# A linear-attention block and a dropless mixture of experts on one core: expert capacity goes from 512 slots each to 896 slots for a pair

## The chip, the cores and the metric

The kernel runs on one core of one Trainium2 chip. The metric is the time of one execution on the device in microseconds, taken over several runs. TensorE (PE in the rows, PEld for its weight loads) does the matrix products, VectorE (DVE), ScalarE (ACT) and GpSimd (POOL) the elementwise work, and SyncE (SP) issues the plain DMAs. GpSimd issues the DMAs whose rows are picked by an index tile.

## The reference, cut to what matters

```python
# gated linear attention: B=4, H=8, S=768, D=48
for t in range(S):
    state = alpha[:, :, t, :, None] * state + k_t (outer) v_t
    y[:, :, t] = einsum('bhd,bhde->bhe', q[:, :, t], state)
x = y.transpose(0, 2, 1, 3).reshape(3072, 384)
# mixture of experts, top 1: E=8, F=1024
expert_idx = argmax(x @ w_gate, axis=1)
gate_w     = softmax(x @ w_gate)[expert_idx]
for e in range(8):                      # rows of expert e only
    h[rows_e]  = maximum(x[rows_e] @ w1[e], 0)    # 384 -> 1024
    y2[rows_e] = h[rows_e] @ w2[e]                # 1024 -> 384
out = gate_w[:, None] * y2
```

For the inputs that are drawn (a fixed seed), the reference gives the eight experts 420, 387, 356, 354, 404, 409, 352 and 390 tokens.

## The kernel before

The program has two stages. The first runs over 24 chunks of 128 tokens: it loads alpha, k, q and v, forms the attention rows as products on TensorE, writes them with their negated logits to a DRAM tensor (`x_rows`), and counts each token into a slot of its expert. Each chunk's steps are issued by hand in a software pipeline (`for s in range(-5, NT + 1)`). `choose` marks the expert of each token of a group of chunks (one to four chunks) in `oh`, `ohs` keeps the running sum over chunks, and `rank_products` and `slots_of` turn them into slot numbers. The slot numbers become one-hot matrices whose products (`tokens_of_slots`) give, for each slot, the number of its token; `indices` makes the index tile `g_idx` of them.

The second stage has the experts. Each has 4 blocks of 128 slots (`NJ = 4`, `CAP = 512`), filled or not; an unused slot points at a row of zeros. For each expert in turn TensorE does three things:

- `turn`: the gathered rows `xg` of a block (128 tokens x 384) are transposed in three 128x128 pieces into a PSUM tile `xtp` (two of them in turn), and VectorE copies it to `xgT`. This is done for the expert that comes next, between the two layers of the present one.
- `layer1`: 8 blocks of hidden units, each 3 products with 512 columns of `xgT` moving (`hp`), then a ReLU on VectorE or ScalarE in turn.
- `layer2`: for each of the 4 token blocks, 8 products in which `w2` moves with 384 columns and 128 columns of `h` are the stationary operand (`zp`); ScalarE scales by the gate, and GpSimd writes the rows out by index.

An f32 product shows as two MATMUL rows in the trace (192 products of layer 1 before: 366 rows with 512 columns and 36 with 256, some for each half of a product that is split in two). The order on each engine is the order of the code (`tc.manual_schedule`). In it `gates` (the gate weights of an expert: two operations on VectorE, an exponential on ScalarE, three more on VectorE) stands ahead of `turn`. For the first expert `begin` does two turns, the first half of three products, then two more turns. The weights come in tiles with three buffers, `w1` and `w2` of an expert 1.5 MB each; those of expert e+3 are requested once `layer2` of e is issued.

Tokens beyond the 512 slots of an expert go to overflow blocks, which a loop after the experts runs one by one (`extra_blocks` sets its count, which is zero when no expert has more than its capacity).

Of the kernel before, what the change touches and what calls it, by code (L numbers as in the profile page):

```python
# [18 lines left out]
def kernel(  # L19
# [22 lines left out]

    nc = tc.nc
    B, H, S, D = q.shape
    C = 128
# [13 lines left out]
    NJ = 4  # L59
    CAP = NJ * C  # L60
    NX = -(-(N - CAP) // C)
    NC = E * NT
    NXB = NT - NJ

# [37 lines left out]
    for name, shape, dt, pattern, base, mult in (  # L102

        ("first_w", [C, E], F32, [[-1, E]], E, 0),

        ("oh_base", [C, E], F16, [[NT, E]], 0, 0),
# [3 lines left out]
        ("thr", [C, NXB], F32, [[C, NXB]], CAP, 0),  # L110
        ("kx", [1, NX], F32, [[1, NX]], 0, 0),
        ("slot_e", [C, E], F32, [[NT * C, E]], 0, 0),
# [4 lines left out]
    first_w, oh_base, iota_h, tokv, thr, kx, slot_e = (iotas[n][1] for n in iotas)  # L117

    def late_consts(i):
# [10 lines left out]
        if i in (2, 3):  # L130
            for ti, tf, pattern, base, mult in list(iotas.values())[4 * (i - 2) : 4 * (i - 1)]:
                nc.gpsimd.iota(ti[:], pattern=pattern, base=base, channel_multiplier=mult)
                nc.gpsimd.tensor_copy(tf[:], ti[:])
            if i == 2:

                nc.sync.dma_start(x_d[N : N + 1, :], zero_w[:])
# [18 lines left out]
    def fetch(ex):  # L155
        w1 = wpool.tile([C, DB, F], F32, name="w1")
        w2 = wpool.tile([C, FB, Dm], F32, name="w2")
        nc.sync.dma_start(w1[:], moe_w1[bass.ds(ex, 1)].rearrange("e (a p) f -> p (e a) f", p=C))
        nc.sync.dma_start(w2[:], moe_w2[bass.ds(ex, 1)].rearrange("e (a p) d -> p (e a) d", p=C))
        return w1, w2  # L160


    with tc.tile_pool(name="ld", bufs=6) as ld, \
# [148 lines left out]
        def choose(g):  # L312
# [8 lines left out]
            nc.vector.tensor_tensor(oh[:, t, :], sc[:], top[:].unsqueeze(2).to_broadcast([C, n, E]), op=ALU.is_equal)  # L321
            for s in g:
                if s == 0:
                    nc.gpsimd.tensor_copy(ohs[:, 0, :], oh_base[:])
                nc.gpsimd.tensor_add(ohs[:, s + 1, :], ohs[:, s, :], oh[:, s, :])
# [8 lines left out]
        def slots_of(g, pos):  # L334
# [5 lines left out]
            with nc.allow_low_precision("a single number is not zero, and it is an integer"):  # L340
                nc.vector.reduce_sum(slot_i[:], own[:], axis=AX)
# [24 lines left out]
        def indices(blocks):  # L366

            n = len(blocks)
            tv = route[:, :NC].rearrange("p (e b) -> p e b", e=E)[:, :, blocks[0] : blocks[-1] + 1]
            gv = g_idx[:].rearrange("p (e b) -> p e b", e=E)[:, :, blocks[0] : blocks[-1] + 1]  # L370
            up = work.tile([C, E, n], F32, name=f"up{n}", bufs=1)
# [19 lines left out]
        for s in range(-5, NT + 1):  # L391
# [27 lines left out]
            if s == 15:  # L419
                w_t[0] = fetch(0)  # L420
# [7 lines left out]
        indices(range(NJ))  # L428
        indices(range(NJ, NT))
# [4 lines left out]
    xg_pool = ctx.enter_context(tc.tile_pool(name="moe_x", bufs=3))  # L434
# [3 lines left out]
    def extra_blocks():  # L438

        cnt = sm.tile([C, E], F32)  # L440
        nc.vector.tensor_tensor(cnt[:], tot[:], slot_e[:], op=ALU.subtract)
        og = sm.tile([C, E, NXB], F32)
        nc.vector.tensor_tensor(
            og[:], cnt[:].unsqueeze(2).to_broadcast([C, E, NXB]), thr[:, None, :].to_broadcast([C, E, NXB]), op=ALU.is_gt,
# [4 lines left out]
        nc.vector.tensor_tensor_scan(ove[:], ovt[:], zero_e[:], 0.0, op0=ALU.add, op1=ALU.add)  # L449
        ended = sm.tile([1, NX, E], F32)  # L450
        ove_b = ove[0:1, None, :].to_broadcast([1, NX, E])
        nc.vector.tensor_tensor(ended[:], ove_b, kx[0:1, :].unsqueeze(2).to_broadcast([1, NX, E]), op=ALU.is_le)
        xf = sm.tile([1, 2 * NX + 1], F32)
        nc.vector.reduce_sum(xf[:, :NX], ended[:], axis=AX)
        nc.vector.tensor_tensor(ended[:], ended[:], ove_b, op=ALU.mult)
        nc.vector.reduce_max(xf[:, NX : 2 * NX], ended[:], axis=AX)
        nc.vector.tensor_scalar_min(xf[:, :NX], xf[:, :NX], float(E - 1))
        nc.vector.tensor_tensor(xf[:, NX : 2 * NX], kx[0:1, :], xf[:, NX : 2 * NX], op=ALU.subtract)
        nc.vector.scalar_tensor_tensor(
            xf[:, NX : 2 * NX], in0=xf[:, :NX], scalar=float(NT), in1=xf[:, NX : 2 * NX], op0=ALU.mult, op1=ALU.add,  # L460
        )
        nc.vector.tensor_scalar(
            xf[:, NX : 2 * NX], xf[:, NX : 2 * NX], scalar1=float(NJ), scalar2=float(NC - 1), op0=ALU.add, op1=ALU.min,
        )
# [3 lines left out]
    def gather(g):  # L468
        g["xg"] = xg_pool.tile([C, NJ, W], F32, name="xg")
        for j in range(g["n"]):  # L470
            nc.gpsimd.indirect_dma_start(  # L471
                out=g["xg"][:, j, :], out_offset=None,
                in_=x_d[:, :], in_offset=bass.IndirectOffsetOnAxis(ap=g["gi"](j), axis=0),
            )

    def gates(g):

        n = g["n"]
        lg = g["xg"][:, :n, Dm:]
        low = wk.tile([C, NJ], F32, name="low")  # L480
        nc.vector.tensor_reduce(low[:, :n], lg, axis=AX, op=ALU.min)
        ex = wk.tile([C, NJ, E], F32, name="ex")
        nc.vector.tensor_tensor(ex[:, :n, :], low[:, :n].unsqueeze(2).to_broadcast([C, n, E]), lg, op=ALU.subtract)
        nc.scalar.activation(ex[:, :n, :], ex[:, :n, :], AF.Exp)
        g["gw"] = wk.tile([C, NJ], F32, name="gw", bufs=3)
        nc.vector.reduce_sum(g["gw"][:, :n], ex[:, :n, :], axis=AX)
        nc.vector.tensor_scalar_add(g["gw"][:, :n], g["gw"][:, :n], 1e-9)
        nc.vector.reciprocal(g["gw"][:, :n], g["gw"][:, :n])

    def turn(g, blocks=None):  # L490
        if blocks is None or blocks[0] == 0:
# [119 lines left out]
```

## Time and profile before

| what | value |
|---|---|
| time, median of 3 runs | 533.97 us (533.76 to 534.03) |
| the profiled execution, its own time | 535.65 us |
| span of that execution | 533.8 us |
| TensorE busy | 498.4 us, 93% of the span |
| weight loads on TensorE | 314.5 us, 59% |
| VectorE, ScalarE, GpSimd busy | 144.4, 107.3, 145.5 us |

The span is what the trace covers; the profiled execution's own time is 1.85 us longer, and 1.68 us above the median of the runs. The attention stage ends near 155 us in the span, the experts begin after a gap at about 166 us, and run to the end.

### The profile page before, as it was taken

To read this page: it belongs to the slowest core of one execution; us is meant where nothing else is said; L and a number is where in the kernel's file an instruction comes from. 1 tells how busy PE (TensorE), PEld (TensorE's weight loads), DVE (VectorE), ACT (ScalarE), POOL (GpSimd) and SP (SyncE) were. 2 spreads that over 40 slices of the span, in tenths; PEclk is the share of its full clock that TensorE was granted. 3 is DMA by queue.
4 is the path that set the end of the run, shared out by engine and by line. 5 is a ranking of instruction groups with operands and counts; after the bars stand their busy time and mean duration, and the time that the engine had idled before them with its cause. 6 is when DMAs were issued, how large, how long until landed. Compare 5 with 4: busy or idle time off the path is not lost.

```text
span 533.8 us, 7442 instructions
## 1 busy us (share of the span) xinstructions
PE 498.4 (93%) x2893; PEld 314.5 (59%) x2893; DVE 144.4 (27%) x399; ACT 107.3 (20%) x217; POOL 145.5 (27%) x229
## 2 busy tenths in 40 slices
PE   4999999999985999999999999999999999999992
PEld 1888888888873645445545544544654554454451
DVE  2435666756782130113012012012001101201100
ACT  3544545444210001010010110101010010011110
POOL 4567454565426201401310130130130010020011
PEclk9999999999995999999999999999999999999997
DMA  8999998889914230503323053050232000000000
GB/s 170 201 186 217 199 217 181 169 262 300 346 47 121 75 114 35 193 9 129 108 100 125 35 178 119 29 190 17 121 136 69 16 29 3 2 33 8 1 29 17
DMA packets 127726, 60.58 MB, mean 113 GB/s; under 512 B 110624, under 2 KB 121951, under 8 KB 127690
## 3 DMA queue, kind: packets, MB, share of 16 engines
q1 hardware_dynamic: 114818, 48.87, 34.0%
q0 software_dynamic: 4096, 11.15, 6.2%
q10 hardware_dynamic: 8776, 0.08, 0.9%
q8 instruction: 24, 0.39, 0.3%
q14 instruction: 12, 0.10, 0.0%
HBM read 50.51 MB, written 11.14 MB: 115 GB/s over the span
## 4 chain that ended last, share of the span: by engine, by line
issue 57%; PE 26%; POOL 10%; DVE 2%; DMA 2%; SPq 1%; ACT 0%; POOLq 0%; ACTq 0%
POOL out_dram L536 6%; PE sA L241 4%; PE y L267 4%; POOL xg L471 4%; PE xr L300 4%; PE tp L228 4%; PE y L261 4%; PE cum L197 3%; PE kvp L278 2%; SPq L181 1%; PE hp L512 1%; DMA a_sb<-in_alpha_dram 1%; DMA xg<-x_rows,g_idx 1%; DMA Eb<-decay_rows 0%; DVE yT L282 0%
## 5 line engine op out<-in xcount | busy, mean ns | idle before, releaser
L512 PE MATMUL hp<-xgT,w 128*128 128x512 f32 (+1 forms) x402 | 169.4, 582 | 1.4 <-DVE xgT L497 1.4
L530 PE MATMUL zp<-w,h_sb 128*128 128x384 f32 x512 | 166.4, 486 | 0.0
L530 PEld LDWEIGHTS zp<-w,h_sb 128*128 128x128 f32 x512 | 96.7, 190 | 66.2 <-issue 0.5
L512 PEld LDWEIGHTS hp<-xgT,w 128*128 128x128 f32 x402 | 78.3, 195 | 89.4 <-issue 83.7
L536 POOL DMA_INDIRECT out_dram<-zo,g_idx x32 | 31.8, 995 | 291.1 <-ACT zo L535 264.8
L506 DVE TENSOR_SCALAR h_sb<-hp 128x512 f32<-128x512 f32 x32 | 22.1, 692 | 261.5 <-PE hp L512 261.5
L535 ACT ACTIVATE zo<-zp,gw 128x384 f32<-128x384 f32 x32 | 18.6, 581 | 166.2 <-PE zp L530 161.6
L508 ACT ACTIVATE h_sb<-hp 128x512 f32<-128x512 f32 x32 | 19.1, 597 | 160.3 <-PE hp L512 160.3
L471 POOL DMA_INDIRECT xg<-x_rows,g_idx x32 | 30.9, 967 | 11.9 <-issue 9.4
L197 PE MATMUL cum<-ln,cmask 128*128 128x384 f32 x48 | 24.1, 586 | 7.9 <-ACT ln L186 4.4
L241 PE MATMUL sB<-qT,kT 48*128 48x128 f32 x192 | 27.7, 285 | 0.0
L241 PE MATMUL sA<-qT,kT 48*128 48x128 f32 x192 | 27.7, 285 | 0.0
L496 PE MATMUL xtp<-ident,xg 128*128 128x128 f32 x96 | 15.4, 291 | 13.1 <-DVE xgT L497 8.6
L228 PEld LDWEIGHTS tp<-ident,kqb 128*128 128x128 f32 x192 | 23.0, 144 | 7.8 <-issue 4.8
L248 POOL TENSOR_SCALAR_AFFINE_SELECT dB<-dB 128x512 f32<-128x512 f32 x24 | 15.3, 638 | 39.9 <-ACT dB L247 26.4
L267 PE MATMUL y<-dB,vb 128*64 128x128 f32 x192 | 26.1, 279 | 0.0
L267 PE MATMUL y<-dA,vb 128*64 128x128 f32 x192 | 26.1, 279 | 0.0
L220 POOL TENSOR_TENSOR kqb<-k_sb,icp 128x384 f32<-128x384 f32 x24 | 24.1, 1002 | 7.4 <-ACT icp L200 7.3
L228 PE MATMUL tp<-ident,kqb 128*128 128x128 f32 x192 | 25.9, 280 | 0.1
L300 PE MATMUL xr<-back,yT 128*128 128x104 f32 x192 | 25.1, 274 | 0.6 <-DVE yT L282 0.4
L241 PEld LDWEIGHTS sA<-qT,kT 48*128 48x128 f32 x192 | 23.1, 187 | 2.5 <-issue 0.3
L221 POOL TENSOR_TENSOR kqb<-q_sb,cp 128x384 f32<-128x384 f32 x24 | 24.0, 1001 | 0.0
(106 smaller groups left out, 414.3 us busy)
## 6 DMA issues: line engine op xcount, KB each, us to landing
w<-in_moe_w_dram SPq DMA_DIRECT2D x16, 1536.0 KB, 7.1
x_rows<-xs SPq DMA_DIRECT2D x24, 196.0 KB, 2.8
a_sb<-in_alpha_dram SPq DMA_DIRECT2D x24, 192.0 KB, 4.0
k_sb<-in_k_dram SPq DMA_DIRECT2D x24, 192.0 KB, 3.8
q_sb<-in_q_dram SPq DMA_DIRECT2D x24, 192.0 KB, 3.8
vb<-in_v_dram SPq DMA_DIRECT2D x24, 192.0 KB, 4.0
Eb<-decay_rows ACTq DMA_DIRECT2D x40, 0.8 KB, 3.1
xg<-x_rows,g_idx POOLq DMA_INDIRECT x32, 3.7
```

Source lines behind the costliest of these rows:

```text
L197: nc.tensor.matmul(cum[:], lhsT=cmask[:], rhs=d["ln"][:], start=True, stop=True)
L220: nc.gpsimd.tensor_tensor(kq[:, 0, :, :D], d["k"][:], heads(d["icp"]), op=ALU.mult)
L221: nc.gpsimd.tensor_tensor(kq[:, 1, :, :D], d["q"][:], heads(d["cp"]), op=ALU.mult)
L228: nc.tensor.transpose(tp[:, p, :], pair(kqb[s % 4][:, i], p), ident[:])
L241: nc.tensor.matmul(t[:, p, :], lhsT=d["kT"][r : r + D, p, :], rhs=d["qT"][r : r + D, p, :], start=True, stop=True,)
L267: nc.tensor.matmul(y[r : r + DP, p, :], lhsT=d["v"][:, 2 * p + i, :], rhs=d["d" + "AB"[i]][:, p, :], start=(c == 0 and p == 0), stop=True, ...
L300: nc.tensor.matmul(xr[:, p, :], lhsT=d["yT"][:, p, :], rhs=back[:, p, :], start=True, stop=True)
L471: nc.gpsimd.indirect_dma_start(out=g["xg"][:, j, :], out_offset=None, in_=x_d[:, :], in_offset=bass.IndirectOffsetOnAxis(ap=g["gi"](j), ax ...
L506: nc.vector.tensor_relu(g["h"][:, f, :cols], hp[:, :cols])
L512: nc.tensor.matmul(hp[:, c0:c1], lhsT=g["w"][0][:, a, f * C : (f + 1) * C], rhs=g["xT"][:, a, c0:c1], start=(a == 0), stop=(a == DB - 1), ...
L530: nc.tensor.matmul(zp[:], lhsT=g["h"][:, f, j * C : (j + 1) * C], rhs=g["w"][1][:, f, :], start=(f == 0), stop=(f == FB - 1),)
L536: ins = nc.gpsimd.indirect_dma_start(out=out[:, :], out_offset=bass.IndirectOffsetOnAxis(ap=g["gi"](j), axis=0), in_=zo[:], in_offset=None ...
```

## The change

Experts are taken in pairs. A pair has 7 blocks of 128 slots (`NJ = 7`); each expert of it has 448 slots (`CAP = 7 * 64`). The first expert's slots count down from the middle of block 3, the second's count up from there. So blocks 0 to 2 belong to the first expert, 4 to 6 to the second, and block 3 is shared, 64 slots each. Counting in two directions is done with a sign per expert (`sgn`, -1 or +1) in `oh`, an absolute value in `slots_of`, and a starting sum (`base2`, placed in `ohs[:, 0, :]`). There are 28 blocks in place of 32, and overflow blocks (21 columns of indices on either side of a pair's 7) start above 448 tokens.

In the expert stage the order for a pair is: `layer1` of the first expert (448 columns), three turns, `gates` for all 7 blocks, `layer2` of blocks 0 to 2, `layer1` of the second expert, four turns for the next pair, `layer2` of the shared block, `layer2` of blocks 4 to 6. The turn of a shared block has two copies, one half for each expert. `layer2` of the shared block has 16 products with 64 stationary columns: those of the first expert write PSUM partitions 0 to 63, those of the second 64 to 127, in alternation.

```diff
-    NJ = 4
-    CAP = NJ * C
+    EP = E // 2
+    NJ = 7
+    HB = C // 2
+    CAP = NJ * HB
...
+            if n == 1:
+                nc.vector.scalar_tensor_tensor(
+                    oh[:, t, :], in0=sc[:], scalar=top[:], in1=sgn[:, None, :], op0=ALU.is_equal, op1=ALU.mult,
+                )
+            else:
+                nc.vector.tensor_tensor(sc[:], sc[:], top[:].unsqueeze(2).to_broadcast([C, n, E]), op=ALU.is_equal)
+                nc.vector.tensor_tensor(oh[:, t, :], sc[:], sgn[:, None, :].to_broadcast([C, n, E]), op=ALU.mult)
...
-                nc.vector.reduce_sum(slot_i[:], own[:], axis=AX)
+                nc.vector.tensor_reduce(slot_i[:], own[:], axis=AX, op=ALU.add, apply_absolute_value=True)
...
+    def turn(xg, j, *to):
+
+        tp = mps.tile([C, DB, C], F32, name="xtp")
+        for a in range(DB):
+            nc.tensor.transpose(tp[:, a, :], xg[:, j, a * C : (a + 1) * C], ident[:])
+        for t, at, c0, c1 in to:
+            nc.vector.tensor_copy(t[:, :, at : at + c1 - c0], tp[:, :, c0:c1])
...
+    def layer2(parts, gw, idx, apart):
+
+        zp = mps.tile([C, Dm], F32, name="zp")
+        m = C // len(parts)
+        for f in range(FB):
+            for i, (w2, h, c0) in enumerate(parts):
                 nc.tensor.matmul(
-                    zp[:], lhsT=g["h"][:, f, j * C : (j + 1) * C], rhs=g["w"][1][:, f, :],
-                    start=(f == 0), stop=(f == FB - 1),
+                    zp[i * m : (i + 1) * m, :], lhsT=h[:, f, c0 : c0 + m], rhs=w2[:, f, :],
+                    start=(f == 0), stop=(f == FB - 1), skip_group_check=True,
                 )
...
+        for p in range(EP):
+            idx = columns(p)
+            a, b = 2 * p, 2 * p + 1
+            xg_next = gather(columns(p + 1)) if p + 1 < EP else None
+            if p == 0:
...
+                for j in range(2):
+                    turn(xg, j, (xTa, j * C, 0, C))
+                begun = [hidden_tile() for _ in range(3)]
+                for f, hp in enumerate(begun):
+                    products1(w_t[0][0], xTa, hp, f, 0, 2 * C)
+                turn(xg, 2, (xTa, 2 * C, 0, C))
+                turn(xg, NH, (xTa, NH * C, 0, HB), (xTb, 0, HB, C))
+            ha = layer1(w_t[a][0], xTa, CAP, begun, 2 * C)
+            begun = ()
+            for j in range(NH + 1, NJ):
+                turn(xg, j, (xTb, HB + (j - NH - 1) * C, 0, C))
+            gw = gates(xg, NJ)
+            w1n = {e: fetch1(e) for e in (a + 3,) if e < E}
+            for j in range(NH):
+                layer2([(w_t[a][1], ha, j * C)], gw[:, j : j + 1], idx[j], True)
+            hb = layer1(w_t[b][0], xTb, CAP)
+            if b + 3 < E:
+                w1n[b + 3] = fetch1(b + 3)
+            if xg_next is not None:
+                xTa = wk.tile([C, DB, CAP], F32, name="xT", bufs=3)
+                xTc = wk.tile([C, DB, CAP], F32, name="xT", bufs=3)
+                for j in range(NH):
+                    turn(xg_next, j, (xTa, j * C, 0, C))
+                turn(xg_next, NH, (xTa, NH * C, 0, HB), (xTc, 0, HB, C))
+                xTb = xTc
+            if p == 0:
                 extra_blocks()
-            layer2(g)
-            if e + 3 < E:
-                w_t[e + 3] = fetch(e + 3)
+            layer2([(w_t[a][1], ha, NH * C), (w_t[b][1], hb, 0)], gw[:, NH : NH + 1], idx[NH], True)
+            if a + 3 < E:
+                w_t[a + 3] = w1n[a + 3], fetch2(a + 3)
+            for j in range(NH + 1, NJ):
+                layer2([(w_t[b][1], hb, HB + (j - NH - 1) * C)], gw[:, j : j + 1], idx[j], True)
+            if b + 3 < E:
+                w_t[b + 3] = w1n[b + 3], fetch2(b + 3)
+            xg = xg_next
```

The order on VectorE at the end of a first layer, before the change (expert 0; `h_sb` is the ReLU, `low`, `ex` and `gw` are the gates, `xgT` the copies of the turns):

```order
L506 TENSOR_SCALAR h_sb<-hp 128x512 x4
L481 TENSOR_REDUCE low<-xg 128x4
L483 TENSOR_TENSOR ex<-low,xg 128x32
L486 TENSOR_REDUCE gw<-ex 128x4
L487 TENSOR_SCALAR gw<-gw 128x4
L488 RECIPROCAL gw<-gw 128x4
L497 COPY xgT<-xtp 128x3x128 x4
```

And with the change, from the first layer of expert 0 to the turns behind the first layer of expert 1 (`xT` are the copies of the turns):

```order
L542 TENSOR_SCALAR h_sb<-hp 128x448 x4
L524 COPY xT<-xtp 128x3x128 x3
L508 TENSOR_REDUCE low<-xg 128x7
L510 TENSOR_TENSOR ex<-low,xg 128x56
L513 TENSOR_REDUCE gw<-ex 128x7
L514 TENSOR_SCALAR gw<-gw 128x7
L515 RECIPROCAL gw<-gw 128x7
L542 TENSOR_SCALAR h_sb<-hp 128x448 x4
L524 COPY xT<-xtp 128x3x128 x3
L524 COPY xT<-xtp 128x3x64 x2
```

The copies of the turns stood behind five operations of the gates; now they stand directly behind the ReLUs, after both layers, and the gates come once per pair behind three of them.

On TensorE, before, the end of the first layer of expert 0 (w_1777 is its `w1` tile), its second layer (w_1778 its `w2` tile, "128x384" is 128 stationary columns and 384 moving ones) and expert 1:

```order
L512 MATMUL hp<-xgT,w_1777 128x512 x15
L496 MATMUL xtp<-ident,xg 128x128 x12
L530 MATMUL zp<-w_1778,h_sb 128x384 x32
L512 MATMUL hp<-xgT,w_2541 128x512 x24
L496 MATMUL xtp<-ident,xg 128x128 x12
```

With the change, the first layer of expert 1, the shared block of the first pair (w_1791 and w_2559 are the `w2` tiles of experts 0 and 1; eight such lines for each) and the second expert's own blocks:

```order
L528 MATMUL hp<-xT,w_2557 128x448 x24
L522 MATMUL xtp<-ident,xg 128x128 x12
L553 MATMUL zp<-w_1791,h_sb 64x384
L553 MATMUL zp<-w_2559,h_sb 64x384
L553 MATMUL zp<-w_1791,h_sb 64x384
L553 MATMUL zp<-w_2559,h_sb 64x384
...
L553 MATMUL zp<-w_2559,h_sb 128x384 x24
L528 MATMUL hp<-xT,w_2561 128x448 x24
```

Of a pair's 7 blocks six have 8 products each as before, and one has 16 products of half the width, the experts in alternation.

## Rows read from the trace of the kernel before

**Rows 1.** The page: the span, and busy time of each engine.
```profile
span 533.8 us, 7442 instructions
PE 498.4 (93%) x2893; PEld 314.5 (59%) x2893; DVE 144.4 (27%) x399; ACT 107.3 (20%) x217; POOL 145.5 (27%) x229
```

**Rows 2.** Windows: stretch, length, busy per engine (instructions), granted clock, DMA share, GB/s.
```profile
20.00:155.00 135.00, 134.42 (x1782) 117.42 (x1780) 84.58 (x220) 59.81 (x127) 73.29 (x146) 1.00 0.90 218
...
170.00:177.60 7.60, 6.81 (x24) 5.34 (x22) 1.02 (x2) 0.00 (x0) 5.77 (x7) 0.67 0.63 161
...
244.00:288.00 44.00, 42.77 (x125) 22.44 (x124) 6.86 (x21) 4.83 (x9) 7.86 (x8) 1.00 0.29 103
```

**Rows 3.** Groups by line and shape: busy us, mean ns of one, idle before.
```profile
L530 PE MATMUL zp<-w,h_sb 128*128 128x384 f32 x512 | 166.4, 486 | 0.0
L512 PE MATMUL hp<-xgT,w 128*128 128x512 f32 x366 | 158.4, 592 | 0.0
...
L267 PEld LDWEIGHTS y<-dA,vb 128*64 128x64 f32 x192 | 20.3, 136 | 3.9 <-issue 2.9 <-DMA q_sb<-in_q_dram 0.2 <-DMA vb<-in_v_dram 0.2
...
L321 DVE TENSOR_TENSOR oh<-sc,top 128x32 f16<-128x32 f32 x4 | 0.8, 192 | 0.1
```

**Rows 4.** Timeline of PE, expert 1: start us, length us, what, count.
```profile
217.97 20.76 PE L512 MATMUL hp<-xgT,w 128*128 128x512 f32 x48
238.57 0.82 PE L496 MATMUL xtp<-ident,xg 128*128 128x128 f32 x6
240.63 1.01 PE L496 MATMUL xtp<-ident,xg 128*128 128x128 f32 x6 [1.23 <-DVE xgT L497]
241.47 0.81 PE L530 MATMUL zp<-w,h_sb 128*128 128x384 f32 x2
```

**Rows 5.** Timeline of DVE, the same place.
```profile
239.52 0.19 DVE L486 TENSOR_REDUCE gw<-ex 128x4 f32<-128x32 f32 x1 [2.31 <-ACT ex L484]
...
240.04 0.99 DVE L497 COPY xgT<-xtp 128x384 f32<-128x384 f32 x2
```

**Rows 6.** Timeline, the last expert's second layer and the end.
```profile
514.00 0.58 ACT L535 ACTIVATE zo<-zp,gw 128x384 f32<-128x384 f32 x1 [4.63 <-PE zp L530]
...
519.16 0.58 ACT L535 ACTIVATE zo<-zp,gw 128x384 f32<-128x384 f32 x1 [4.58 <-PE zp L530]
...
525.17 0.98 POOL L536 DMA_INDIRECT out_dram<-zo,g_idx  x1 [4.17 <-ACT zo L535]
```

**Rows 7.** Timeline, the first expert: gathers, third and fourth turn, products.
```profile
170.65 0.94 POOL L471 DMA_INDIRECT xg<-x_rows,g_idx  x1 [0.30 <-issue]
...
175.97 0.82 PE L496 MATMUL xtp<-ident,xg 128*128 128x128 f32 x6
176.49 1.02 DVE L497 COPY xgT<-xtp 128x384 f32<-128x384 f32 x2 [7.49 <-PE xtp L496]
177.57 5.01 PE L512 MATMUL hp<-xgT,w 128*128 128x256 f32 x20 [0.79 <-DVE xgT L497]
```

**Rows 8.** Timeline of PE in one chunk: products in two halves of the array.
```profile
102.44 0.37 PE L241 MATMUL sA<-qT,kT 48*128 48x128 f32 x1
...
102.66 0.27 PE L241 MATMUL sA<-qT,kT 48*128 48x128 f32 x1
...
104.72 0.27 PE L267 MATMUL y<-dA,vb 128*64 128x128 f32 x1
104.72 0.27 PE L267 MATMUL y<-dB,vb 128*64 128x128 f32 x1
104.82 0.27 PE L267 MATMUL y<-dA,vb 128*64 128x128 f32 x1
```

**Rows 9.** DMA issues on the page (KB each, median us to landing), and one request.
```profile
w<-in_moe_w_dram SPq DMA_DIRECT2D x16, 1536.0 KB, 7.1
...
xg<-x_rows,g_idx POOLq DMA_INDIRECT x32, 3.7
...
194.63 0.38 SPq L158 DMA_DIRECT2D w<-in_moe_w_dram  x1
```

More of the change, by code (lines that the diff above doesn't have):

```diff
@@ L116 @@
         )
[L117 removed]
+    first_w, iota_h, tokv, sgn, slot0, base2, thr, kx, xcol = (iotas[n][1] for n in iotas)
     def late_consts(i):
@@ L465, in extra_blocks, with gather @@
+        nc.vector.tensor_tensor(nth[:], nth[:], per(xcol), op=ALU.add)
+        nc.vector.tensor_tensor(nth[:], nth[:], live[:], op=ALU.mult)
+        nc.vector.reduce_sum(xf[:, NX : 2 * NX], nth[:], axis=AX)
         nc.vector.tensor_copy(xf[:, 2 * NX :], ove[0:1, E - 1 :])
         nc.vector.tensor_copy(xe[:], xf[:])
-    def gather(g):
-        g["xg"] = xg_pool.tile([C, NJ, W], F32, name="xg")
-        for j in range(g["n"]):
+    def gather(idx):
+        xg = xg_pool.tile([C, len(idx), W], F32, name="xg")
+        for j, i in enumerate(idx):
@@ L514, in products1, with hidden_tile @@
                 start=(a == 0), stop=(a == DB - 1), skip_group_check=True,
             )
[L517 to L529 removed]
+    def hidden_tile():
+        return mps.tile([C, CAP], F32, name="hp", bufs=3)
@@ new lines, in layer2 @@
+        zo = wk.tile([C, Dm], F32, name="zo", bufs=3)
+        nc.scalar.activation(zo[:], zp[:], AF.Copy, scale=gw)
+        ins = nc.gpsimd.indirect_dma_start(
+            out=out[:, :], out_offset=bass.IndirectOffsetOnAxis(ap=idx, axis=0),
+            in_=zo[:], in_offset=None, bounds_check=N - 1, oob_is_err=False,
+        )
+        if apart:
+            ins = getattr(ins, "ins", ins)
+            tc.declare_no_dep(ins, group="rows_out", reason="disjoint rows")
+            tc.add_to_no_dep_group("rows_out", ins)
@@ L576 @@
             nc.vector.tensor_copy(gi[:], g_idx[:, bass.ds(col, 1)])
-            g = dict(n=1, w=fetch(ex), gi=lambda j: gi[:], apart=False)
-            gather(g)
-            turn(g)
-            gates(g)
-            layer1(g)
-            layer2(g)
+            w1, w2 = fetch1(ex), fetch2(ex)
+            xg = gather([gi[:]])
+            gw = gates(xg, 1)
+            xT = wk.tile([C, DB, CAP], F32, name="xT", bufs=3)
+            turn(xg, 0, (xT, 0, 0, C))
+            h = layer1(w1, xT, C)
+            layer2([(w2, h, 0)], gw[:, 0:1], gi[:], False)
 _INS = ['q', 'k', 'v', 'alpha', 'moe_w_gate', 'moe_w1', 'moe_w2']
```

183 lines of the change are left out of this document (77 added, 106 removed).

## Prediction

> **What bounds the kernel now.** I read the page first: TensorE is busy 93% of the span and no other engine passes 27%, weight loads apart [rows 1]. An average over two stages doesn't say where a cut pays, so the windows come next. In the attention stage TensorE is busy 134.42 of 135 us, VectorE 84.58 and GpSimd 73.29; in the expert stage TensorE has 42.77 of 44 us while VectorE has 6.86 and GpSimd 7.86 [rows 2]. Both stages are bound by TensorE, the expert stage with over 30 us of 44 free on each other engine. The groups by shape name what fills it: 512 rows of `zp` and 366 full rows of `hp`, together 325 us, with no idle time before them [rows 3]. So columns taken from these products come off the end, if nothing new waits.
>
> The timeline then gives the unit. Expert 1's first layer runs from 217.97 to 238.57, 20.60 us; the turns from 238.57 to 241.47, 2.90 us; blocks of the second layer are 519.16 - 514.00 = 5.16 us apart by their evictions [rows 4, 6]. 20.60 + 2.90 + 4 x 5.16 = 44.14 us an expert. Every term of the sum is a piece of this.
>
> **Layer 1, 512 to 448 columns.** A row of it takes 20.60 / 48 = 429.2 ns for 512 columns; a row of `zp` takes 5.16 / 16 = 322.5 ns for 384 [rows 4, 6]. The 128 columns between them are worth 106.7 ns, so 64 are worth 53.3 ns. 48 rows x 8 experts x 53.3 ns = **20.5 us off**. The first expert's split products lose their 64 columns from the second half, which starts at 177.57, behind the stretch whose granted clock averages 0.67 [rows 2, 7]; I keep the same price there.
>
> **Layer 2, 32 blocks to 28.** Of each pair's 8 blocks one goes: 4 x 5.16 = **20.6 us off**, if the shared block, with its 16 products, costs what 8 cost. That rests on two products running side by side in two halves of the array's columns. The attention stage has such products: dA and dB, 128 partitions in, 64 columns each, start together at 104.72, and the next pair 0.10 us later at 104.82 [rows 8]. A row of 128 columns alone is worth 106.7 ns by the slope above. So a pair costs as much as one, though both halves have moving data of their own from all 128 partitions, as here. The bound on the other side, no overlap, is 4 x 5.16 = 20.6 us given back. I take the overlap, since the nearest rows are of the same kind and differ only in the moving length.
>
> Going into such pairs costs a little: in front of the scores the second pair starts 0.22 us after the first (102.44, 102.66), where 0.107 is the price [rows 8]. That is 0.11 us; with as much on the way out and four blocks, **0.9 us on**. Bounds: 0 and, if it doubles, 1.8.
>
> **Turns.** Here is a gain that the sizes don't show. Twelve transposes take four times 0.41 us (six take 0.82), but the turns last 2.90 us, because the seventh to twelfth have to wait for `xtp`: TensorE idles 1.23 us for the copy `xgT` [rows 4]. The copy in turn starts only at 240.04, 1.47 us after the transposes, as VectorE sits in the gates, 2.31 us idle for ScalarE's exponential, which itself stands behind the last ReLU [rows 5]. In the changed order the copies stand behind the ReLUs alone. Rows without gates ahead show what that gives: transposes at 175.97, copy at 176.49 (0.52 later), two copies in 1.02, and the product that needs them 0.06 after their end, at 177.57 [rows 7]. So the third turn starts at 0.52 + 0.51 + 0.06 = 1.09 us, and three turns take 1.09 + 0.41 = 1.50 us. The fourth starts one copy later, at 1.60, and four take 2.01 us. Nothing behind them waits: the next layer-2 block needs only `h`. Before: 7 x 2.90 = 20.3 us. After: four sets of three and three of four, 4 x 1.50 + 3 x 2.01 = 12.0 us. **8.3 us off.** Bounds: if a turn keeps its 2.90 / 4 = 0.725 us, the 24 of them behind the start take 17.4 and 2.9 us come off; at 0.41 us each it would be 10.5.
>
> The gates now stand behind three turns. Their exponential still waits for the last ReLU, but the first eviction that needs the gate comes a block (5.16 us) later, and ScalarE is busy 4.83 of 44 us [rows 2]. If that cover were gone, each of four gates would cost the 1.2 us that it costs now.
>
> **What is hidden.** In `choose` the sign costs VectorE one more operation for each of six groups, 0.19 us [rows 3], some 1.2 us in a stage where it has 50 us free [rows 2]; a group's slots are asked for a chunk later. Where a group has one chunk, as the last three have, the sign shares an instruction with the comparison, so the chain ahead of the first gather stays as long. Uncovered, the six would cost 1.2 us. The index tile is 196 columns for 192: nothing I can price above 0.1 us. The additional iotas on GpSimd fall in chunks where it is half idle. The overflow count grows by a few small VectorE operations behind the first pair's turns, with no eviction due on VectorE until the next first layer. At the start, the first product waits for turns 0 and 1 as before; the copy of the fourth turn has two halves, and the first product behind it needs one: 0.2 us off, within the rounding.
>
> **DMAs.** The requests for `w1` move forward, behind the first layers, and those for `w2` back, behind the shared block or the pair's end. On SP's queue a `w2` now stands behind a `w1` that waits for the next first layer. The first request was at 194.63 and a tile lands in 7.1 us [rows 9]; each tile of the new order is asked for a whole pair (2 x 18.0 + 7 x 5.16 + 3.5, some 76 us) ahead of its use, the last-placed `w2` included. The seventh gather is issued at 170.65, and lands in 3.7 us [rows 7, 9]; block 6 is turned after a first layer that runs to about 192 (177.57, 18 rows of 160 ns, 30 of 376). Later pairs ask for 7 gathers a pair ahead. No wait here.
>
> **Sum.** -20.5 - 20.6 - 8.3 + 0.9 - 0.2 = -48.7 us. The profiled execution took 535.65 us (span 533.8), so one like it would take 487.0, with a span of 485.1. The median of the runs is 1.68 us below the profiled one: 533.97 - 48.7 = **485.3 us**.
>
> **Rivals.** (a) *The turns keep their stall*, because copies and ReLUs still meet on VectorE: 5.4 us less gain, 490.7 us. The order speaks against it, but 1.09 us is put together from three rows. 10%.
>
> (b) *The weight loads of the shared block show.* The two halves share rows of the array, and if a 64-column load (136 ns [rows 3]) could not run under the other half's product, each of 16 passes x 4 blocks would grow by it: 8.7 us, giving 494.0. Against it stands the pair period of 0.10 us, in which loads of 136 ns are hidden [rows 3, 8]. 6%. On this the Trainium skill, "TensorE: Matmul & The Clock Gate", section "Part 3: Packing small matmuls — row/col tiling", says that a weight load overlaps with a running product only where the row group differs; by that rule the time would be that of (b). The trace disagrees: dA and dB use the same 128 rows.
>
> (c) *No overlap with 384 moving columns*: the shared block takes 10.3 us, 505.9 us. Against it the same rows. 5%.
>
> (d) *Slower than before: overflow.* A block beyond an expert's 448 slots runs alone behind the experts: two weight tiles (7.1 us each on landing, the second partly under the first), a gather (3.7), 24 products of 128 columns (48 x 0.107 = 5.1 us), one second-layer block (5.2) and the write: some 25 us with nothing beside it. From two such blocks on the kernel is slower: 485.3 + 50 = 535 us. The counts speak against it: the largest expert has 420 tokens of 448. 2%, with any other loss of that size.
>
> **How the numbers follow.** 74% for the forecast, 10, 6, 5 and 2% for (a) to (d), 3% for a loss that I don't see, between 1 and 30 us. The forecast's own range is 483.5 to 487.5, from the bounds of the column switch and the turns (2.2 us faster, a little over 1 us slower by rounding and scatter). For 8 in 10 and more, with the cost bounds of (a) and (b), the range is 483.0 to 494.5. A difference of 0.2%, about what a measurement of this kernel can tell from no change, is 1.1 us; nothing but (d) or a mix of losses comes near it: faster 97%, same 1%, slower 2%.
>
> **What would show it.** First layers of 18.0 us with rows 376 ns apart; the shared block's eviction 5.2 to 5.5 us behind its start (10.3 for (c), 7.3 for (b)); turns of 1.5 and 2.0 us, with idle for the copy near 0.3 and 0.4 us in place of 1.23; no change before 177 us; the last write issued 8.6 us ahead of the span's end, as now (525.17 of 533.8 [rows 1, 6]). A granted clock below 1.00 in a shared block, or TensorE idle for a weight tile, would make the sum wrong.

## The result, and the profile after

The changed kernel takes 489.86 us, the median of 4 runs (489.16 to 490.76), beside 533.94 us for the kernel before (4 runs, 533.76 to 534.03): a ratio of 0.918, interval 0.916 to 0.919. The gain is 44.1 us, where 48.7 were forecast. The profiled execution took 489.74 us with a span of 488.0; against the profiled execution of before, its span is 45.8 us shorter, and this is the difference that the two traces can take apart.

The page of the changed kernel: the span, then busy time of each engine, then one line of its DMA queues (packets, MB, share of 16 engines' span).

```profile
span 488.0 us, 7370 instructions
...
PE 457.6 (94%) x2881; PEld 297.4 (61%) x2881; DVE 142.3 (29%) x391; ACT 103.2 (21%) x209; POOL 137.8 (28%) x226
...
q1 hardware_dynamic: 114818, 48.87, 39.6%
```

TensorE lost 40.8 us of busy time [rows 1] and still fills the span. The groups by line and shape of the changed kernel say which rows carry that:

```profile
L528 PE MATMUL hp<-xT,w 128*128 128x448 f32 x366 | 138.9, 539 | 0.0
L553 PE MATMUL zp<-w,h_sb 128*128 128x384 f32 x384 | 125.6, 487 | 0.0
L553 PE MATMUL zp<-w,h_sb 128*64 128x384 f32 x128 | 21.5, 489 | 0.0
...
L553 PEld LDWEIGHTS zp<-w,h_sb 128*64 128x64 f32 x128 | 8.8, 137 | 11.2 <-issue 11.2
```

`hp` went from 158.4 to 138.9 us and `zp` from 166.4 to 147.1 [rows 3]. The third line is the shared block: 128 rows of half the width are busy for 21.5 us together, 5.4 us for each of four blocks, while a row by itself still lasts 489 ns. That is 168 ns of busy time a row, where a row of full width has 327 (125.6 us for 384): they run two at a time.

The timeline of TensorE in the first pair, from the turns behind the first layer of expert 0 to the first layer of expert 2:

```profile
194.84 0.82 PE L522 MATMUL xtp<-ident,xg 128*128 128x128 f32 x6
195.98 0.55 PE L522 MATMUL xtp<-ident,xg 128*128 128x128 f32 x3 [0.32 <-DVE xT L524]
196.37 15.65 PE L553 MATMUL zp<-w,h_sb 128*128 128x384 f32 x48
211.85 18.20 PE L528 MATMUL hp<-xT,w 128*128 128x448 f32 x48
229.89 0.82 PE L522 MATMUL xtp<-ident,xg 128*128 128x128 f32 x6
231.03 1.01 PE L522 MATMUL xtp<-ident,xg 128*128 128x128 f32 x6 [0.32 <-DVE xT L524]
231.97 21.06 PE L553 MATMUL zp<-w,h_sb 128*64 128x384 f32 x80
252.87 7.30 PE L528 MATMUL hp<-xT,w 128*128 128x448 f32 x19
```

Starts subtracted from starts give the units: a first layer 229.89 - 211.85 = 18.04 us; three turns 196.37 - 194.84 = 1.53; four turns 231.97 - 229.89 = 2.08, with one wait of 0.32 for the copy, where 1.23 stood before [rows 4]; four blocks, the shared one among them, 252.87 - 231.97 = 20.90. ScalarE's eviction of the shared block:

```profile
237.43 0.58 ACT L558 ACTIVATE zo<-zp,gw 128x384 f32<-128x384 f32 x1 [6.79 <-PE zp L553]
```

The shared block is evicted 237.43 - 231.97 = 5.46 us behind its start.

So far the profile is as forecast. What isn't stands ahead of the experts. The timeline of the changed kernel from the last routing product to the third turn:

```profile
164.13 0.21 PE L443 MATMUL cum<-ohs,ones_sq 128*128 128x8 f16 x1
...
164.63 0.19 DVE L391 SCALAR_TENSOR_TENSOR g_idx<-cum,up 128x28 int32<-128x28 f32 x1
...
165.59 0.15 DVE L449 COPY tot<-cum 128x8 f32<-128x8 f32 x1
166.67 1.21 POOL L499 DMA_INDIRECT xg<-x_rows,g_idx  x1 [3.96 <-issue]
...
179.13 0.82 PE L522 MATMUL xtp<-ident,xg 128*128 128x128 f32 x6
```

The same places in the kernel before:

```profile
161.91 0.21 PE L425 MATMUL cum<-ohs,ones_sq 128*128 128x8 f16 x1
...
162.89 1.19 POOL L471 DMA_INDIRECT xg<-x_rows,g_idx  x1 [2.41 <-DVE up L372]
```

The last routing product is 2.22 us later. The first gather follows it after 0.98 us before, and after 2.54 us now, although its index columns (`g_idx`) are written by 164.82. In place of a releaser the row of after has "issue": the profile shows nothing that GpSimd waited for. And the last write of the changed kernel:

```profile
480.17 0.98 POOL L559 DMA_INDIRECT out_dram<-zo,g_idx  x1 [4.18 <-ACT zo L558]
```

Cut at these events, the difference of the two spans is:

| stretch | before | after | difference |
|---|---|---|---|
| start to the last routing product | 161.91 | 164.13 | +2.22 |
| to the first gather | 0.98 | 2.54 | +1.56 |
| to the third turn | 13.08 | 12.46 | -0.62 |
| to the last write | 349.20 | 301.04 | -48.16 |
| to the end of the span | 8.63 | 7.83 | -0.80 |
| span | 533.8 | 488.0 | -45.8 |

The experts gave 48.16 us for 48.7 forecast; the start took back 3.16, and the end gave 0.80. The medians lie 1.7 us closer than the two spans, since the profiled execution of before was 1.7 us above its median and that of after was not.

### The profile page after: what moved, and what is told of

Read it like the earlier page. It is cut to its first block, busy times and chain, and to the rows that moved or that the text cites. A ratio compares the mean times of both kernels' runs of the same rounds, so it can differ in the third digit from the quotient of the medians.

```text
span 488.0 us, 7370 instructions
## 1 busy us (share of the span) xinstructions
PE 457.6 (94%) x2881; PEld 297.4 (61%) x2881; DVE 142.3 (29%) x391; ACT 103.2 (21%) x209; POOL 137.8 (28%) x226
## 3 DMA queue, kind: packets, MB, share of 16 engines
q1 hardware_dynamic: 114818, 48.87, 39.6%
## 4 chain that ended last, share of the span: by engine, by line
issue 54%; PE 27%; POOL 11%; DVE 2%; DMA 2%; SPq 1%; ACT 0%; POOLq 0%; ACTq 0%
POOL out_dram L559 6%; POOL xg L499 5%; PE sA L254 5%; PE y L280 4%; PE tp L241 4%; PE xr L313 4%; PE cum L210 4%; PE y L274 4%; PE kvp L291 2%; SPq L194 1%; DMA a_sb<-in_alpha_dram 1%; DMA x_rows<-xs 1%; DVE yT L295 1%; DVE sc L330 0%; DVE dA L258 0%
## 5 line engine op out<-in xcount | busy, mean ns | idle before, releaser
L528 PE MATMUL hp<-xT,w 128*128 128x448 f32 (+2 forms) x402 | 148.4, 530 | 1.2 <-DVE xT L524 1.2
L553 PE MATMUL zp<-w,h_sb 128*128 128x384 f32 (+1 forms) x512 | 146.8, 488 | 0.0
L528 PEld LDWEIGHTS hp<-xT,w 128*128 128x128 f32 x402 | 77.4, 194 | 69.9 <-issue 65.0
L553 PEld LDWEIGHTS zp<-w,h_sb 128*128 128x128 f32 (+1 forms) x512 | 81.1, 177 | 62.4 <-issue 13.6
L559 POOL DMA_INDIRECT out_dram<-zo,g_idx x28 | 27.7, 988 | 251.7 <-ACT zo L558 251.7
L542 DVE TENSOR_SCALAR h_sb<-hp 128x448 f32<-128x448 f32 x32 | 20.0, 624 | 218.4 <-PE hp L528 218.4
L544 ACT ACTIVATE h_sb<-hp 128x448 f32<-128x448 f32 x32 | 17.4, 543 | 142.0 <-PE hp L528 142.0
L558 ACT ACTIVATE zo<-zp,gw 128x384 f32<-128x384 f32 x28 | 16.3, 581 | 133.6 <-PE zp L553 129.0
L499 POOL DMA_INDIRECT xg<-x_rows,g_idx x28 | 26.9, 960 | 12.2 <-issue 12.2
L313 PEld LDWEIGHTS xr<-back,yT 128*128 128x128 f32 x192 | 23.3, 192 | 1.5 <-issue 1.0
```

Of the source, the lines that this page charges most:

```text
L313: nc.tensor.matmul(xr[:, p, :], lhsT=d["yT"][:, p, :], rhs=back[:, p, :], start=True, stop=True)
L499: nc.gpsimd.indirect_dma_start(out=xg[:, j, :], out_offset=None, in_=x_d[:, :], in_offset=bass.IndirectOffsetOnAxis(ap=i, axis=0),)
L528: nc.tensor.matmul(hp[:, c0:c1], lhsT=w1[:, a, f * C : (f + 1) * C], rhs=xT[:, a, c0:c1], start=(a == 0), stop=(a == DB - 1), skip_group_c ...
L542: nc.vector.tensor_relu(h[:, f, :cols], hp[:, :cols])
L553: nc.tensor.matmul(zp[i * m : (i + 1) * m, :], lhsT=h[:, f, c0 : c0 + m], rhs=w2[:, f, :], start=(f == 0), stop=(f == FB - 1), skip_group_ ...
L559: ins = nc.gpsimd.indirect_dma_start(out=out[:, :], out_offset=bass.IndirectOffsetOnAxis(ap=idx, axis=0), in_=zo[:], in_offset=None, bound ...
```

## The experiments

Two questions were open: do the three terms in the experts (columns, blocks, turns) have the causes that the prediction gave them, and why does the first gather come later. Unless it says otherwise an edit is made on the changed kernel. Each ratio is against the kernel before on the same chip.

**Gates behind the turns, in the kernel before.** `e1_gates_behind_turns` moves one call:

```diff
-            gates(g)
             ... (the four turns)
+            gates(g)
```

> The kernel before with one edit: in each expert the gates stand behind the turns, not ahead of them. Theory: the 1.23 us for which TensorE waits in each set of four turns comes from the gates that stand ahead of the copies on VectorE; then a set takes 2.0 us in place of 2.9, seven times, and the time falls by 6.2 us to 527.7 us. Rival: the copies are late for want of a PSUM tile or by their own length; then the time stays at 533.9 us.

It took 528.88 us (527.38 to 529.37, 4 runs), ratio 0.988 (0.986 to 0.990), 6.04 us off. TensorE at the end of expert 1's first layer, to be laid beside [rows 4]:

```profile
237.66 0.82 PE L496 MATMUL xtp<-ident,xg 128*128 128x128 f32 x6
238.80 1.01 PE L496 MATMUL xtp<-ident,xg 128*128 128x128 f32 x6 [0.32 <-DVE xgT L497]
239.65 20.81 PE L530 MATMUL zp<-w,h_sb 128*128 128x384 f32 x64
```

Four turns take 1.99 us in place of 2.90, seven times 0.91 = 6.4 us by the rows, and the wait is the 0.32 us of the changed kernel. The stall was the place of the gates on VectorE; no part of the pairing is needed to remove it.

**Gates ahead of the turns, in the changed kernel.** `e4_gates_ahead` puts it back, four times in the run:

```diff
+            gw = gates(xg, NJ)
             for j in range(NH + 1, NJ):
                 turn(xg, j, (xTb, HB + (j - NH - 1) * C, 0, C))
-            gw = gates(xg, NJ)
```

> The changed kernel with the gates ahead of the three turns behind the first layer of a pair, as the order was before. Theory: the copies then wait for ScalarE's exponential again, which stands behind the last ReLU; three turns take about 2.4 us in place of 1.5, four times: 3.8 us longer, 493.7 us. Rival: with 7 blocks to a gate and one fewer turn the stall is hidden; then 489.9 us.

It took 492.19 us (491.83 to 492.55, 4 runs), ratio 0.920 (0.918 to 0.922). The time alone doesn't tell it from the changed kernel, whose ratio was 0.917 to 0.921 in three series; the rows do:

```profile
193.99 0.82 PE L522 MATMUL xtp<-ident,xg 128*128 128x128 f32 x6
196.03 0.55 PE L522 MATMUL xtp<-ident,xg 128*128 128x128 f32 x3 [1.23 <-DVE xT L524]
196.41 15.65 PE L553 MATMUL zp<-w,h_sb 128*128 128x384 f32 x48
```

The 1.23 us wait is back to the hundredth; three turns take 2.42 us in place of 1.53, and from the third turn to the last write it is 304.65 us in place of 301.04, 3.6 for four sets.

**The two halves in sequence.** `e2_halves_in_sequence` has the same 16 products of 64 columns in another order:

```diff
-        for f in range(FB):
-            for i, (w2, h, c0) in enumerate(parts):
+        for i, (w2, h, c0) in enumerate(parts):
+            for f in range(FB):
```

> The changed kernel with the shared block's 16 products in another order: the 8 of the first expert, then the 8 of the second, in place of alternation. Theory: the shared block is cheap because neighbouring products sit in different halves of the array; then in this order it takes 10.3 us in place of 5.2, four times, and the time is 20.6 us longer, 510.5 us. Rival: a product of 64 columns is cheap by itself (half the columns, half the time); then nothing changes, 489.9 us.

It took 504.81 us (one run); third turn to last write 316.73 us, 15.7 more. Its group of half-width rows, TensorE's rows from the shared block on, two of its weight loads, and the eviction:

```profile
L553 PE MATMUL zp<-w,h_sb 128*64 128x384 f32 x128 | 37.2, 489 | 0.0
...
231.36 24.98 PE L553 MATMUL zp<-w,h_sb 128*64 128x384 f32 x80
...
234.96 0.14 PEld L553 LDWEIGHTS zp<-w,h_sb 128*64 128x64 f32 x1 [0.19 <-issue]
235.28 0.84 PEld L553 LDWEIGHTS zp<-w,h_sb 128*64 128x64 f32 x7 [0.18 <-issue]
...
240.70 0.58 ACT L558 ACTIVATE zo<-zp,gw 128x384 f32<-128x384 f32 x1 [10.68 <-PE zp L553]
```

The group is busy 37.2 us in place of 21.5, and the block is evicted 9.34 us behind its start in place of 5.46. Half a width of columns alone buys nothing: within one half the loads come one in 0.32 us, the time of a whole row of 384 columns. Only where the halves change, at 235.28, seven loads come together: the last rows of the first half ran beside the first of the second. That is why it lost 15.7 and not the 20.6 of no overlap. What the alternation is worth here is the difference of the two evictions, 3.88 us a block.

**One overflow block.** `e5_one_overflow_block` lets one expert count an overflow block, which runs and holds no token:

```diff
-        ("thr", [C, NX], F32, [[C, NX]], CAP, 0),
+        ("thr", [C, NX], F32, [[C, NX]], CAP - 30, 0),
```

> The changed kernel with the limit from which an overflow block is counted lowered by 30 slots, to 418, so that one expert (420 tokens) has one; the block itself finds no tokens left and writes no rows, so the output is the same. It measures what a block in the loop behind the experts costs. By the working of the prediction some 25 us: 515 us. If the loop's own cost (branches, waits of all engines) is large, 35 us and more.

It took 509.81 us (one run); third turn to last write 321.78, 20.7 more. Its timeline at the end:

```profile
480.56 0.99 POOL L499 DMA_INDIRECT xg<-x_rows,gi  x1 [1.00 <-issue]
...
484.58 0.90 PE L522 MATMUL xtp<-ident,xg 128*128 128x128 f32 x3 [6.95 <-DMA xg<-x_rows,gi]
...
486.13 7.11 PE L528 MATMUL hp<-xT,w 128*128 128x128 f32 x48 [0.65 <-DVE xT L524]
...
493.08 5.33 PE L553 MATMUL zp<-w,h_sb 128*128 128x384 f32 x16
...
499.30 1.00 POOL L559 DMA_INDIRECT out_dram<-zo,gi  x1 [17.75 <-ACT zo L558]
```

What TensorE waits for is the gather; the weights aren't in the chain, so the 7 us that I had counted for them did not show. They came long before: between 385 and 415 us the DMA engines moved 3.1 MB more than in the changed kernel (236 and 127 GB/s in the two halves of this window, for 132 and 22), the size of the block's two weight tiles. Its 128-column products take 493.08 - 486.13 = 6.95 us where I had 5.1. The windows over them show why (columns as in [rows 2]; the granted clock is the third figure from the end):

```profile
484.00:488.00 4.00, 2.77 (x12) 2.37 (x12) 1.46 (x7) 0.21 (x1) 0.00 (x0) 0.50 0.00 1
...
490.00:493.00 3.00, 3.00 (x30) 3.00 (x29) 0.80 (x3) 0.55 (x2) 0.00 (x0) 1.00 0.00 0
```

Behind its wait of 6.95 us for the gather TensorE ran at a granted clock of 0.50, the lower of its two levels, and of 1.00 by 490, where 30 rows pass in 3.00 us, near the 107 ns a row of the prediction. The kernel gains 44 us on these inputs. By this price, which is an estimate from one block in one run, two such blocks (41.4) would take nearly all of it back and three make it slower; a second block was not measured, and whether its weights would come as early is open.

**The later gather: which columns it waits for, and how much VectorE has to do.** The first theory was that the gather waits for the whole index tile, which the change writes in three parts. `e3_own_index_tile` gives a pair's 7 main columns a tile of their own:

```diff
+    g_mid = rte.tile([C, EP, NJ], I32)
...
+            if blocks[0] == NX:
+                gv = g_mid[:]
...
-        c0 = p * PB + NX
-        return [g_idx[:, c0 + j : c0 + j + 1] for j in range(NJ)]
+        return [g_mid[:, p, j : j + 1] for j in range(NJ)]
```

> The changed kernel with the index columns of the 7 main blocks in a tile of their own, so that a gather depends on the first of the three index steps alone. Theory: in the changed kernel the first gather waits for the two steps behind it, since their columns lie on either side of those it reads (index step done at 164.82, the copy behind the last at 165.74, the gather at 166.67); then it starts 0.3 us after its own index step, and 1.5 us come off: 488.3 us. Rival: the gather waits for the last write of rows to DRAM, which lands at about that time; then nothing changes, 489.8 us.

`e6_sign_on_gpsimd` takes the sign's operation off VectorE, `e7_both` makes both edits, and `e0_after_again` is the changed kernel, on the same chip in the same series.

```diff
-                nc.vector.tensor_tensor(oh[:, t, :], sc[:], sgn[:, None, :].to_broadcast([C, n, E]), op=ALU.mult)
+                nc.gpsimd.tensor_tensor(oh[:, t, :], sc[:], sgn[:, None, :].to_broadcast([C, n, E]), op=ALU.mult)
```

> The changed kernel with the sign's additional operation, for the six groups of several chunks, on GpSimd in place of VectorE. Theory: in the changed kernel the chain of choose on VectorE delays the copy yT, and with it the products xr (TensorE idle 0.5 us at 50 us, more in small pieces); then 0.3 to 0.7 us come off: 489.3 us. Rival: the delay comes from VectorE operations that stand against GpSimd's (a comparison of 1.33 us for 0.31), not from their number; then the time stays within 0.3 us of the changed kernel's, or grows, as GpSimd has more to do.

> Both of the edits (own index tile, the sign on GpSimd). If both theories hold, 1.8 to 2.2 us less than the changed kernel: 487.8 us. If the edits interact nowhere, the two differences add up.

> The changed kernel once more, as the mark for the three beside it. The profile of it showed the expert stage 48.2 us shorter, as forecast (48.7), but its start 3.2 us later (third turn at 179.13 for 175.97). Theory: about 1.4 us of that is the first loads of the program, which differ from execution to execution; then a second profile has the attention stage's chunks at other times in the first 20 us, by up to 1.4 us either way. Rival: all of it belongs to the change; then the second profile has them at the same times within 0.2 us. Time 489 to 490.5 us.

| kernel | median, us | runs | ratio |
|---|---|---|---|
| `e0_after_again` | 490.41 | 490.17 to 493.68 | 0.917 (0.914 to 0.920) |
| `e3_own_index_tile` | 492.00 | 490.57 to 493.57 | 0.920 (0.917 to 0.922) |
| `e6_sign_on_gpsimd` | 492.59 | 490.33 to 494.09 | 0.920 (0.917 to 0.923) |
| `e7_both` | 491.35 | 490.18 to 493.38 | 0.919 (0.916 to 0.922) |

Nothing is gained. With its own index tile the gather still starts 2.50 us behind the last routing product (163.41, 165.91); with the sign on GpSimd that product comes at 163.32, beside 163.47 for the changed kernel in this series. Both theories fell.

**The later gather: where its rows land.** In the addresses of the built programs the buffers of `xg` lie inside the freed landing tiles of the attention stage before the change; with it the second of them reaches 576 bytes per partition into the first tile of the pool `work`, which other engines use too. The theory was that the gather has to wait for these engines. `e8_rows_first` exchanges two pools, so that `xg` lies inside the landing tiles again; `e9_rows_first_own_index` adds the index tile of `e3`.

```diff
-    sm = ctx.enter_context(tc.tile_pool(name="moe_sm", bufs=1))
     ... (the pool of xg)
+    sm = ctx.enter_context(tc.tile_pool(name="moe_sm", bufs=1))
```

> The changed kernel with the pool of the gathered rows placed ahead of the small tiles of the expert stage, nothing else. Theory: in the changed kernel the rows' tiles of 7 blocks lie on memory of the attention stage that is let go late, so that the first gather waits for all of VectorE's index work and two engines more (gather 1.86 us behind its index step, 0.29 before); in this place it waits for VectorE alone, and starts within 0.9 us of its index step: the distance from the last product of the routing to the first gather falls from 2.50 to 1.0 to 1.6 us, and with it the start of the experts. 1 to 1.5 us off the time on the same chip. Rival: the wait is for the three index steps as such; then 2.50 us stay.

> The same, with the 7 main columns in an index tile of their own. Theory: with the memory out of the way the gather depends on its own index step alone and starts 0.3 us behind it, 0.95 us behind the last product of the routing, as before the change; 1.5 us off the time. Rival: no difference to the placement alone.

> The kernel before, once more, for a second profile on the chip of the three beside it. If the later start of the changed kernel's experts (third turn at 177.5 to 179.1 in six profiles, for 176.0 in two of kernels before the change) belongs to the change, the third turn stands near 176 here too; if it is the chip or the execution, at 177.5 or later. Time 534 to 536 us.

> The changed kernel on the same chip, as the mark for the placement: 489 to 492 us, gather 2.50 us behind the last product of the routing.

| kernel | median, us | runs | ratio | product to gather, us |
|---|---|---|---|---|
| `e11_after_mark`, the changed kernel | 492.97 | 491.29 to 494.07 | 0.921 (0.918 to 0.923) | 2.50 |
| `e8_rows_first` | 490.44 | 489.65 to 492.73 | 0.917 (0.914 to 0.919) | 0.99 |
| `e9_rows_first_own_index` | 490.09 | 489.05 to 492.72 | 0.916 (0.913 to 0.919) | 0.95 |
| `e10_before_again`, the kernel before | 536.1 | one run | | 0.98 |

The rows of `e8_rows_first`:

```profile
163.35 0.21 PE L443 MATMUL cum<-ohs,ones_sq 128*128 128x8 f16 x1
...
164.34 1.21 POOL L499 DMA_INDIRECT xg<-x_rows,g_idx  x1 [2.41 <-DVE up L390]
```

The gather is back at 0.99 us, with the releaser that it had before the change (the index step). So the order of the two pools, and with it the place of the `xg` buffers, is the cause of the 1.56 us. That the 576 bytes are, is argued from the addresses: the first tile asked of `work` is `ln`, whose last reader in the changed kernel's profile ended at 132.3 us, so no row shows it in use at 165. What that is worth at the end is less plain: the medians of this series are 2.5 and 2.9 us below the changed kernel, but the ratio of the changed kernel itself was 0.918, 0.917 and 0.921 in three series, a scatter of 2 us on 490. `e9_rows_first_own_index` has the lowest median of its series; that it beats the changed kernel by more than this scatter isn't shown.

`e10_before_again` has its last routing product at 161.49, its gather at 162.47, its third turn at 175.68. A third profile with the old blocks, `e1_gates_behind_turns`, has them at 162.70, 163.64 and 175.95. In the eleven profiles of the changed kind the last routing product comes at 163.27 to 164.13, and in the nine whose gather is late the third turn comes at 177.5 to 179.1. So the late start belongs to the change, but the pair of profiles in the table shows nearly its largest size: 2.22 us for the routing product, where the nearest two profiles are 0.57 apart, and 3.16 for the third turn, where they are 1.55 apart.

## Why the prediction was right, and where it was off

The gain came out 4.6 us smaller than forecast, and 489.86 us is outside the forecast's own 483.5 to 487.5. (By the words that stand with it, 2.2 us faster and a little over 1 slower, that range would be 483.1 to some 486.5.) It is inside the wide range of 483.0 to 494.5, but that one was widened for rivals (a) and (b), and neither occurred. That it held is luck in this: 489.86 stands close to the 490.7 of rival (a), though the turns came as forecast. What occurred is what the prediction called "a loss that I don't see" and gave 3%. The 4.6 us are 0.5 in the experts and 3.2 at their start, less 0.8 at the end, and 1.7 for the distance of the profiled execution of before from its median, which the forecast took off for both kernels and the changed one does not have.

**Layer 1, 20.5 us: right.** 18.04 us a layer, 375.8 ns a row, where 18.0 and 376 were forecast. 8 x (20.60 - 18.04) = 20.5 us. The 0.2 us at the first products came too: they start 1.41 us behind the third turn (179.13, 180.54), 1.60 before [rows 7].

**Layer 2, 20.6 us off and 0.9 on: right.** The shared block and the three behind it take 20.90 us, 0.26 more than 4 x 5.16: 1.0 us for four pairs. The shared block is evicted 5.46 us behind its start, in the forecast's 5.2 to 5.5. Rival (b) is out: loads of 137 ns that showed would have put the eviction at 7.3 us. The Trainium skill, "TensorE: Matmul & The Clock Gate", section "Part 3: Packing small matmuls — row/col tiling", says that a weight load overlaps with a running product only where the row group differs. The trace disagrees: both halves use all 128 rows, and still only 5.46 us pass. Rival (c) is out too; `e2_halves_in_sequence` shows what stood behind it: the overlap came only where neighbours in the order lie in different column halves.

**Turns, 8.3 us: right in cause, 0.4 too high.** 7 x 2.90 - 4 x 1.53 - 3 x 2.08 = 7.9 us. Two experiments show the cause from both sides, 6.04 us off where the gates go behind the turns, 3.6 on where they go ahead again. Rival (a) is out.

**The start of the experts: the step that failed.** In "What is hidden" the prediction had "the chain ahead of the first gather stays as long", and in its list of signs "no change before 177 us". The third turn came at 179.13 in place of 175.97. I had counted the operations of the chain, and these are indeed no longer. Two things that aren't operations moved instead. One is shown: 1.56 us because of where the buffers of the gathered rows were placed. The other is 2.22 us by which the attention stage ends later. At the sixth chunk 1.36 of them are there already: its product `cum` starts at 23.22 us, 21.86 before. `e0_after_again` was to say whether this changes from execution to execution: there it starts at 23.00, in all eleven profiles of the changed kind at 22.97 to 23.52, and in the two others of the old blocks at 21.45 (`e10`) and 22.67 (`e1`). So theory and rival of that run hold in part: with the old blocks the executions differ by more than 1 us, and yet the two kinds stay apart, by 0.3 us where they come nearest. The windows of the first loads, before and then after (columns as in [rows 2]):

```profile
4.00:8.00 4.00, 1.62 (x3) 0.51 (x3) 0.58 (x3) 1.54 (x4) 0.35 (x1) 1.00 1.06 206
8.00:12.00 4.00, 2.55 (x4) 1.10 (x5) 0.00 (x0) 1.28 (x3) 2.85 (x4) 1.00 0.98 193
```

```profile
4.00:8.00 4.00, 1.62 (x2) 0.50 (x2) 0.51 (x3) 0.70 (x3) 0.00 (x0) 1.00 1.29 194
8.00:12.00 4.00, 1.66 (x3) 0.51 (x3) 0.00 (x0) 2.02 (x5) 2.31 (x3) 1.00 1.36 186
```

The DMA engines are busier and move less (the share, next to last, adds the times of all packets, so it can pass 1). Over the whole run the same 48.87 MB in the same 114818 packets take 39.6% of 488.0 us = 193 us of the 16 engines, and took 34.0% of 533.8 = 181 us. Every changed kernel that loads these bytes shows this (38.7 to 40.2% at spans of 488 to 503 us), and the three profiles of the old blocks the other (34.0 to 34.6% of 527 to 534). It isn't the whole of the delay: `e1` has the DMA time of the old blocks (34.6% of 527.4 us) and its sixth chunk nearly as late as the changed kernel. Which loads became dearer, and why, isn't settled. In the built programs the landing tiles of the attention stage, filled in runs of 192 bytes, start 32 bytes past a multiple of 64 with the change and on one before it; that this is the cause is only argued, and a kernel with these tiles moved by 32 bytes wasn't run.

How far the third turn moves hangs on the granted clock too. TensorE waits for the first gather and starts the experts at 0.50, and how soon it has 1.00 again differs. Over the second stretch of [rows 2] the mean is 0.50 in the changed kernel's first profile:

```profile
170.00:177.60 7.60, 6.64 (x18) 4.89 (x19) 1.11 (x2) 0.00 (x0) 5.77 (x7) 0.50 0.56 157
```

In `e0` and `e11` it is 0.60 and 0.65, and the 18 rows of the first half products, which end in this stretch or just behind it, take 6.04 and 5.67 us where they take 6.56 in that profile.

**The end, 0.8 us that the forecast didn't have.** The tail behind the last write is 7.83 us in place of 8.63, where the forecast kept 8.6. Two closing steps on GpSimd's queue carry it, before and then after (ns, shortest, median and longest):

```profile
L571 POOLq INC_SWDGE_SEM  x1: 1452/1452/1452, 526.2 to 526.2; - x1
L606 POOLq DRAIN  x3: 45/107/5293, 527.7 to 533.5; - x3
```

```profile
L623 POOLq INC_SWDGE_SEM  x1: 1292/1292/1292, 481.2 to 481.2; - x1
L659 POOLq DRAIN  x3: 40/107/4652, 482.5 to 487.7; - x3
```

They are 0.16 and 0.64 us shorter, together the 0.80. GpSimd issued 64 gathers and writes before and 56 with the change; with the overflow block of `e5`, 58, the long drain lasts 4.82 us. That is 0.083 us for each DMA at all three counts, though no run varied the count alone.

**What stays open.** In seven profiles of the changed kind the first ReLU of expert 0 starts 3.0 to 4.7 us behind the start of the second half products that it needs, where four have 1.28. One kernel shows both: the changed kernel in the last series (`e11_after_mark`), and its first profile, where these products start at 180.54:

```profile
179.75 3.19 PE L528 MATMUL hp<-xT,w 128*128 128x192 f32 x18 [1.28 <-issue]
...
184.30 0.62 DVE L542 TENSOR_SCALAR h_sb<-hp 128x448 f32<-128x448 f32 x1 [4.33 <-PE hp L528]
```

```profile
181.82 0.62 DVE L542 TENSOR_SCALAR h_sb<-hp 128x448 f32<-128x448 f32 x1 [1.07 <-PE hp L528]
```

Those seven (`e0`, `e3`, `e6` to `e9`, `e11`) have nothing else changed in the experts, and take 301.8 to 305.7 us from the third turn to the last write, in place of 301.04. They are all the kernels of the changed kind in two of the three series of experiments; in the third (`e2`, `e4`, `e5`) and in the first profile none has it. Behind that first layer they agree: from its end to the last write the seven take 285.34 us and the first profile 285.33. In `e11` the wait is followed by a second stretch at the lower granted clock, and thirty rows of this layer take 13.24 us for 11.54 in `e0`:

```profile
185.50:188.90 3.40, 3.40 (x6) 1.60 (x5) 0.62 (x1) 0.54 (x1) 0.00 (x0) 0.50 0.00 1
```

So what the profiled executions of the changed kernel differ by lies ahead of that layer's end. What holds the ReLUs there isn't known.

**Overflow, rival (d).** It did not occur with these inputs; a first block costs 20.7 us in place of the 25 that I had put together. Its weights are no part of the chain; the lower granted clock, which I hadn't counted, gave 2 us of that back.

## What to carry to other kernels

Two sets of products whose stationary operands fill half the columns each cost here about one set of full width, with moving data and weights of their own, when they stood in alternation (5.46 us to the eviction, for 5.16 a full block); in sequence they took 9.34. When TensorE waits for a copy, look at what stands ahead of the copy on the copying engine: an order of calls that is correct either way was worth 6 of 534 us. And when an edit changes the size or order of tiles, look at where pools now lie over each other, not only at the operations: here the order of two pools was worth 1.56 us in a wait that no row names.

## What was not expected of the hardware

A wait of 1.56 us that goes away when two pools change places shows as "issue", with no releaser. The rows of the half-width block last 489 ns each, as long as full ones (487), and the pair of them still takes one's time. The same bytes in the same packets took 193 us of the DMA engines' time in one kernel and 181 in the other. Behind a wait of 6.95 us in an otherwise full program TensorE restarted at a granted clock of 0.50, which cost the overflow block some 2 us (6.95 for its first layer in place of 5.1). And the program's end got 0.80 us shorter with eight indirect DMAs fewer.
